# One load of a DMA-bound GroupNorm moved to the GpSimd queue, over fifteen DMA engines instead of sixteen

## The chip, the cores and the metric

The kernel runs on one core of one Trainium2 chip. The metric is the device time of one execution in microseconds (us). The page counts sixteen DMA engines on the core, and in the traces a large transfer posts sixteen landings whichever queue issues it (SyncE's stores below; GpSimd's load in the changed kernel, from 287.9 to 300.8 us).

## The reference

```python
# x: (128, 1024, 32, 16) bf16, G = 32 groups of 32 channels; g, b: (1024,)
xr = x.reshape(B, G, C // G, H, W)
mu = xr.mean(axis=(2, 3, 4), keepdims=True)
var = ((xr - mu) ** 2).mean(axis=(2, 3, 4), keepdims=True)
xn = (xr - mu) / jnp.sqrt(var + 1e-5)
return xn.reshape(B, C, H, W) * g[None, :, None, None] + b[None, :, None, None]
```

It reads 134 MB and writes 134 MB, and it computes little. Moving those bytes is the whole problem.

## The kernel before

The tensor is cut into 32 tiles of 128 rows (4 images times 32 groups). A row is 16,384 bf16 values, 32 KB in one piece. Six tile buffers rotate: five or six loads are in flight ahead of the computing, and a store releases a buffer for a load six tiles later. All large transfers go out on the SyncE queue.

```python
XBUFS = 6
UPFRONT = 6
AHEAD = 5
...
def L(i):                                   # load of tile i
    xt = xpool.tile([P, F], BF16, name="xt")
    parts = NQ if i == 0 or i >= NT - 1 else 1
    w = F // parts
    for c in range(parts):
        chain("sp", nc.sync.dma_start(out=xt[:, c*w:(c+1)*w], in_=x_v[i][:, c*w:(c+1)*w]))
    state[i] = {"xt": xt}
...
for i in range(NT):
    Q(i)                                    # ScalarE: sums of squares
    if i + 1 < NT:
        M(i + 1); R0(i + 1)                 # TensorE and VectorE: sums
    V(i)
    for c in range(NQ):
        A(i, c)                             # VectorE: 8 tensor_scalar of 128x512, in place
        ...
    if not in_parts:
        S(i, 0, NQ)                         # store of tile i, SyncE queue
    j = i + AHEAD
    if UPFRONT <= j < NT:
        L(j)
```

## Time and profile before

| | before |
|---|---|
| time, median of its first 3 runs | 638.12 us |
| DMA engines busy | 9 tenths or more in 39 of 40 slices |
| ScalarE, VectorE, TensorE busy | 79%, 65%, 45% |
| one row of 32 KB on one DMA engine | 1.213 us |

These lines are from the page of the kernel before: the span, the DMA busy row and the GB/s row (one entry for each fortieth of the span), the DMA queues, and the chain of work that ended last.

```profile
span 636.1 us, 3995 instructions
...
DMA  9999999999999999999999999999999999999993
GB/s 373 443 430 398 429 434 432 441 429 431 431 428 433 433 437 427 434 429 429 433 431 436 433 433 431 431 430 435 433 433 435 430 431 429 437 418 439 428 422 151
...
q1 hardware_dynamic: 10944, 268.44, 98.3%
q8 instruction: 8, 0.13, 0.1%
q14 instruction: 15, 0.12, 0.0%
...
DMA 80%; ACT 11%; issue 2%; DVE 2%; PE 1%; SPq 1%; DVEq 0%; ACTq 0%
```

The engines never rest and move about 430 GB/s in the middle of the run; q1 is the SyncE queue. q8 and q14 carry instructions, not data: 23 packets, a quarter of a megabyte.

An average over sixteen engines hides the one that is late. Every large transfer posts sixteen increments to its semaphore, and the trace has their times. They are read here as one from each engine: two loads in a row landed 9.7 us apart in all sixteen (22.4 to 22.8, then 32.1 to 32.5 us), which is eight rows of 1.213 us. In the fence below, the sixteen landing times in us, sorted, of three transfers of the kernel before (taken from the trace's landings, not a view of the page):

```
load landing first at  22.4:  22.4  22.4  22.4  22.4 ...  22.6  22.6  22.8
load landing first at 284.5: 284.5 284.6 284.6 284.8 ... 287.0 288.3 289.2 290.2
last store:                  623.7 623.8 624.0 624.2 624.3 625.3 625.6 625.6
                             625.7 625.8 625.9 626.5 628.1 628.8 628.8 635.1
```

The spread grows from 0.5 to 11.4 us. At the end one engine is alone, 6.3 us behind the next. The kernel ends when that one does.

### The profile page before, as it was taken

Reading aid. Unit: us, or ns where it says so; the run is one execution under the profiler, and the core shown is the slowest. Engines: PE = TensorE matmul, PEld = TensorE weight load, DVE = VectorE, ACT = ScalarE, POOL = GpSimd, SP = SyncE. Lnnn points to the kernel's source line nnn. Section 1 sums busy time; section 2 is a strip of 40 time slices with the busy share of each in tenths; the row PEclk is TensorE's granted clock in tenths of the full one; section 3 lists DMA queues with packets and bytes.
Section 4 is the critical chain, followed back from the end, with each engine's and each line's share of the span. In section 5 each row is a group of like instructions: output and inputs, shape, how many; then the busy total and the mean of one; then the engine's idle time right before and its main releaser. Section 6 shows DMA issues by size and latency. Waiting matters only on the chain.

```text
span 636.1 us, 3995 instructions
## 1 busy us (share of the span) xinstructions
PE 288.7 (45%) x1025; PEld 113.2 (18%) x1025; DVE 412.6 (65%) x1371; ACT 499.8 (79%) x298; POOL 0.8 (0%) x6
## 2 busy tenths in 40 slices
PE   5567604563335642356433555425553445546000
PEld 2223201221112210122111222112221112212000
DVE  1388888886686665875567756677555785668740
ACT  4899999997886777977679767797767986779920
POOL 0000000000000000000000000000000000000000
PEclk9789758766788666887567875678765787668655
DMA  9999999999999999999999999999999999999993
GB/s 373 443 430 398 429 434 432 441 429 431 431 428 433 433 437 427 434 429 429 433 431 436 433 433 431 431 430 435 433 433 435 430 431 429 437 418 439 428 422 151
DMA packets 11063, 268.70 MB, mean 422 GB/s; under 512 B 1312, under 2 KB 1312, under 8 KB 1312
## 3 DMA queue, kind: packets, MB, share of 16 engines
q1 hardware_dynamic: 10944, 268.44, 98.3%
q8 instruction: 8, 0.13, 0.1%
q14 instruction: 15, 0.12, 0.0%
q10 hardware_dynamic: 96, 0.00, 0.0%
HBM read 134.22 MB, written 134.22 MB: 422 GB/s over the span
## 4 chain that ended last, share of the span: by engine, by line
DMA 80%; ACT 11%; issue 2%; DVE 2%; PE 1%; SPq 1%; DVEq 0%; ACTq 0%
DMA out_dram<-xt 72%; ACT ja L228 11%; DMA xt<-in_x_dram 8%; DVE xt L305 1%; PE pa L162 1%; SPq L98 1%; DVE jv L245 0%; ACT rstd L258 0%; DVE rstd L266 0%; DVEq L372 0%; DVE bia L277 0%; DVE scl L271 0%; DVE jd L177 0%; ACTq L228 0%; SPq L318 0%
## 5 line engine op out<-in xcount | busy, mean ns | idle before, releaser
L228 ACT ACTIVATE ja<-xt,q 128x4096 bf16<-128x4096 bf16 x128 | 474.2, 3704 | 9.9 <-DVE jd L177 6.8
L305 DVE TENSOR_SCALAR xt<-xt,scl,bia 128x512 bf16<-128x512 bf16 x1016 | 333.5, 405 | 1.2
L162 PE MATMUL pa<-xt,eye 128*128 128x512 bf16 x256 | 109.8, 607 | 298.8 <-DMA xt<-in_x_dram 298.8
L162 PEld LDWEIGHTS <-eye 128*128 128x128 bf16 x1024 | 113.1, 113 | 474.4 <-DMA xt<-in_x_dram 300.2
L162 PE MATMUL pb<-xt,eye 128*128 128x512 bf16 x768 | 184.9, 400 | 1.0 <-DMA xt<-in_x_dram 1.0
L177 DVE TENSOR_SCALAR_CACHE_REDUCE jd<-pa 128x512 bf16<-128x512 f32 x32 | 22.1, 689 | 155.8 <-PE pa L162 155.8
L258 ACT ACTIVATE rstd<-var,eps_t 128x1 f32<-128x1 f32 x32 | 9.4, 294 | 96.4 <-DVE jv L245 96.4
L228 ACT ACTIVATION_READ_ACCUMULATOR ja<-xt,q 128x1 f32 x128 | 23.9, 186 | 0.0
L177 DVE TENSOR_SCALAR_CACHE_REDUCE jd<-pb,q 128x512 bf16<-128x512 f32 x32 | 23.7, 741 | 0.0
L245 DVE TENSOR_SCALAR_CACHE_REDUCE jv<-sq,seed 128x4 f32<-128x4 f32 x32 | 6.8, 214 | 18.9 <-ACT ja L228 18.9
L266 DVE RECIPROCAL rstd<-rstd 128x1 f32<-128x1 f32 x32 | 5.2, 164 | 11.6 <-ACT rstd L258 11.6
L277 DVE SCALAR_TENSOR_TENSOR bia<-scl,negmean,gb 128x32 f32<-128x32 f32 x32 | 8.0, 251 | 1.1
L271 DVE TENSOR_SCALAR scl<-gb,rstd 128x32 f32<-128x32 f32 x32 | 7.7, 242 | 1.1
L198 DVE TENSOR_SCALAR off<-negmean,q 128x1 f32<-128x1 f32 x32 | 6.8, 214 | 1.1
L298 ACT ACTIVATE xt<-xt,bia,scl 128x512 bf16<-128x512 bf16 x8 | 5.8, 800 | 0.8 <-DVE bia L277 0.8
L210 DVE SCALAR_TENSOR_TENSOR seed<-off 128x1 f32<-128x1 f32 x32 | 5.1, 159 | 1.1
L153 DVE COPY gb<-gb_p 128x64 f32<-128x64 f32 x1 | 0.2, 225 | 5.3 <-PE gb_p L145 5.3
L245 DVE DVE_READ_ACCUMULATOR jv<-sq,seed 128x1 f32 x32 | 2.6, 83 | 0.0
L177 DVE DVE_READ_ACCUMULATOR jd<-pa 128x1 f32 x32 | 2.6, 82 | 0.0
L113 ACT ACT_TABLE_LOAD x1 | 1.3, 1283 | 1.7 <-PEq L361 1.7
L177 DVE DVE_READ_ACCUMULATOR jd<-pb,q 128x1 f32 x32 | 2.5, 80 | 0.0
L111 DVE MEMSET eps_t<- 128x1 f32 x1 | 0.1, 59 | 0.9 <-PEq L361 0.9
(10 smaller groups left out, 1.7 us busy)
## 6 DMA issues: line engine op xcount, KB each, us to landing
xt<-in_x_dram SPq DMA_DIRECT2D x30, 4096.0 KB, 29.7
out_dram<-xt SPq DMA_DIRECT2D x30, 4096.0 KB, 39.1
xt<-in_x_dram SPq DMA_DIRECT2D x8, 1024.0 KB, 16.8
out_dram<-xt SPq DMA_DIRECT2D x8, 1024.0 KB, 25.3
gb_b<-in_g_dram ACTq DMA_DIRECT2D x1, 2.0 KB, 3.3
gb_b<-in_b_dram ACTq DMA_DIRECT2D x1, 2.0 KB, 5.3
```

The costliest lines, as they stand in the source:

```text
L98: nc.sync.dma_start(out=xt[:, c * w : (c + 1) * w], in_=x_v[i][:, c * w : (c + 1) * w]),
L162: nc.tensor.matmul(out=ps[:], lhsT=eye[:], rhs=st["xt"][:, k * MMN : (k + 1) * MMN], start=(k == lo), stop=(k == hi - 1),),
L177: nc.vector.tensor_scalar(out=jd[:], in0=ps[:], scalar1=-inv_n, scalar2=seed, op0=ALU.mult, op1=ALU.add, accum_out=total[:],),
L198: nc.vector.tensor_scalar(out=off[:], in0=st["negmean"][:], scalar1=1.0 / NQ, scalar2=st["q"][:], op0=ALU.mult, op1=ALU.subtract,),
L228: nc.scalar.activation(out=ja[:], in_=st["xt"][:, k * QF : (k + 1) * QF], func=ACT.Square, bias=st["q"][:], scale=1.0 / NQ, accum_out=sq[: ...
L245: nc.vector.tensor_scalar(out=jv[:], in0=st["sq"][:], scalar1=inv_n, scalar2=st["seed"][:], op0=ALU.mult, op1=ALU.add, accum_out=var[:],),
L258: nc.scalar.activation(out=rstd[:], in_=var[:], func=ACT.Sqrt, bias=eps_t[:], scale=float(NQ * NQ),),
L266: chain("dve", nc.vector.reciprocal(out=rstd[:], in_=rstd[:]))
L271: nc.vector.tensor_scalar(out=scl[:], in0=gam, scalar1=rstd[:], scalar2=None, op0=ALU.mult),
L277: nc.vector.scalar_tensor_tensor(out=bia[:], in0=scl[:], scalar=st["negmean"][:], in1=bet, op0=ALU.mult, op1=ALU.add,),
L298: nc.scalar.activation(out=span, in_=span, func=ACT.Identity, bias=bia, scale=scl),
L305: nc.vector.tensor_scalar(out=span, in0=span, scalar1=scl, scalar2=bia, op0=ALU.mult, op1=ALU.add,),
```

## The change

The intent is to give the late engine less to do. Each engine normally carries eight of a tile's 128 rows (the 9.7 us above). For tile 16, rows 0 to 119 are issued from GpSimd, meant for fifteen engines with eight rows each, so that one takes none; rows 120 to 127 go out from SyncE. Two tiny loads of the weights `g`, whose data nobody reads, are there to set which engine GpSimd's load leaves out.

```diff
+SPLIT_TILE = 16
+WIDE = 120
+SPARED = 4
...
+    def turn(n):
+        t = consts.tile([n, 4, 4], BF16, name=f"turn{n}")
+        chain("pool", nc.gpsimd.dma_start(
+            out=t[:, :, 0:2],
+            in_=g[0 : n * 8].rearrange("(p a c) -> p a c", a=4, c=2)))
+
     def L(i):
         xt = xpool.tile([P, F], BF16, name="xt")
+        if i == SPLIT_TILE:
+            chain("pool", nc.gpsimd.dma_start(
+                out=xt[0:WIDE, :], in_=x_v[i][0:WIDE, :], max_dma_last_dim=F))
+            chain("sp", nc.sync.dma_start(out=xt[WIDE:P, :], in_=x_v[i][WIDE:P, :]))
+            turn(16 - SPARED)
+            state[i] = {"xt": xt}
+            return
...
     for i in range(min(UPFRONT, NT)):
         L(i)
+
+    turn(SPARED + 1)
```

More of the change, by code (lines that the diff above doesn't have):

```diff
@@ L89 @@
     state = {}
+    def turn(n):
+        t = consts.tile([n, 4, 4], BF16, name=f"turn{n}")
+        chain(
+            "pool",
+            nc.gpsimd.dma_start(
+                out=t[:, :, 0:2],
+                in_=g[0 : n * 8].rearrange("(p a c) -> p a c", a=4, c=2),
+            ),
+        )
     def L(i):
         xt = xpool.tile([P, F], BF16, name="xt")
+        if i == SPLIT_TILE:
+            chain(
+                "pool",
+                nc.gpsimd.dma_start(
+                    out=xt[0:WIDE, :], in_=x_v[i][0:WIDE, :], max_dma_last_dim=F
+                ),
+            )
+            chain("sp", nc.sync.dma_start(out=xt[WIDE:P, :], in_=x_v[i][WIDE:P, :]))
+            turn(16 - SPARED)
+            state[i] = {"xt": xt}
+            return
         parts = NQ if i == 0 or i >= NT - 1 else 1
```

## The prediction

The places marked as cut, here and in the expectations below, held statements that no trace or run of this case shows: how queues choose their engines, what in the hardware makes rows slow each other, and what a load from GpSimd might cost.

> **What bounds the kernel now.** The DMA engines. On the page, the busy row is 9 in 39 of 40 slices, q1 fills 98.3% of 16 engines' span at a mean 422 GB/s, and the chain of work that ended last is 80% DMA, 11% ACT. ACT (79%) and DVE (65%) have slack.
>
> The sixteen engines are not alike. Every large transfer posts sixteen landings in the trace. They spread over 0.5 us at the first tiles, 5.7 us by 290 us, and 11.4 us at the last store: first 623.7, then 628.1, 628.8, 628.8, and one alone at 635.1. So one engine is 6.3 us behind the next two, and the program waits for it. Its lag grows in steps of about 1 us (at 251, 310, 360, 418, 468, 527, 576 us); the 8 KB instruction packets of q14 start just before (242, 301, 358, 416, 459, 517, 574 us). I read it as the engine that fetches one compute engine's instructions. Packets carry no engine number; followed end to start, the late engine was the fifth to start, which fits engine 4 but proves nothing.
>
> **What the change does.** Each engine moves 8 rows of 32 KB per tile, 1.213 us a row. For tile 16, 120 rows go from GpSimd over fifteen engines, 8 each; the last 8 rows from SyncE. [...] So engine 4 carries 1 row instead of 8: 7 x 1.213 = 8.5 us less[...]. No run here shows this placement yet[...].
>
> **Critical path.** All of the late engine's excess is on it. After, the late engine ends at 635.1 - 8.5 = 626.6; the next, 628.8 (630.0 with an extra row), becomes last. Gain at most 5.1 to 6.3 us.
>
> Costs: [...] A late start of this load hurts little: its tile's store is issued about 49 us after it lands (290 to 339 us), while computing takes about 29. The engines then hold at least 8 us of queued work, so none should starve.
>
> **Prediction.** 633.8 us (-0.7%); 80% range 631.2 to 639.5. Faster by over 2%: 1%; within 2%: 98%; slower by over 2%: 1%.
>
> **What would show it.** Right: after the load of tile 16 the gap between last and second-last landing (1.7 us at 310) vanishes; the last store's gap falls from 6.3 to under 1.5 us; the first landings move under 2 us. The GpSimd load lands within 35 us of issue.
>
> **What would make it wrong.** Engine 4 is not the late one[...]: the gap stays about 6 us and the time is 638 to 640. Or GpSimd's load is slow[...]: all sixteen landings shift by several microseconds and the gain is eaten.

In numbers, the forecast's sum was 638.1 us, less the gain of 5.1 to 6.3 us, plus a cost of 1 to 2 us on every engine: 632.8 to 635.0, put at 633.8. The cost term came from no run. The extra row of 1.213 us, for the eight engines that take the last eight rows, is in the 630.0. That engine 4 takes one row was an assumption too; the traces showed later that the eight-row load posts its landings at 279.2, 284.7 to 286.3 (six of them) and 295.3 us, the engine that runs ahead and the late one among them. As for the 8 us of queued work, the trace of before has 13.6 us for the earliest engine at 280.6 us, when the load of the next tile was issued: it ended its part of the last transfer queued by then at 294.2.

## The result, and the profile after

The changed kernel took 642.83 us (median of 4 runs, 641.93 to 643.41), against 638.11 us before (4 runs): a ratio of 1.0072, 95% interval 1.0054 to 1.0089. Ratios here are the mean time of one kernel's fast runs over that of the other's fast runs of the same rounds, so they are not quite the ratio of the medians. The outcome is within 2%, but on the wrong side, and outside the predicted range.

The same lines of the page of the changed kernel:

```profile
span 641.7 us, 4006 instructions
...
DMA  9999999999999999999999999999999999999992
GB/s 382 433 424 406 437 426 428 434 439 427 427 433 437 429 431 434 421 358 411 436 429 428 438 433 429 431 436 431 429 436 435 432 429 431 435 418 440 424 426 106
...
q1 hardware_dynamic: 10816, 264.51, 96.3%
q0 software_dynamic: 336, 3.93, 1.7%
q8 instruction: 8, 0.13, 0.1%
q14 instruction: 15, 0.12, 0.0%
...
DMA 79%; ACT 11%; issue 2%; PE 2%; DVE 2%; SPq 1%; DVEq 0%; ACTq 0%
```

The busy row is as full as before, and the chain by engines reads the same to a per cent. (By lines it doesn't: it now runs through tile 16's load, and the loads' share of it is 14% instead of 8%.) The GB/s row shows a dent in slices 17 to 19 (421, 358, 411), where tile 16 is loaded; q0 is GpSimd's queue. The view of busy time by stretches says where in the dent. Its columns are the stretch, its length, then TensorE, weight load, VectorE, ScalarE and GpSimd busy, the granted clock, the DMA busy share and GB/s; here before:

```profile
262.00:278.00 16.00, 7.11 (x24) 2.84 (x25) 9.46 (x33) 11.93 (x8) 0.00 (x0) 0.68 1.00 430
278.00:288.00 10.00, 2.08 (x10) 0.76 (x8) 9.93 (x32) 9.90 (x7) 0.00 (x0) 0.87 1.00 429
288.00:300.00 12.00, 9.75 (x32) 3.72 (x32) 5.67 (x21) 8.09 (x6) 0.00 (x0) 0.68 1.01 434
```

and after:

```profile
262.00:278.00 16.00, 3.00 (x9) 1.04 (x8) 7.43 (x24) 10.29 (x6) 1.33 (x2) 0.59 1.00 417
278.00:288.00 10.00, 5.92 (x26) 2.40 (x24) 8.68 (x30) 8.28 (x6) 0.00 (x0) 0.97 1.02 324
288.00:300.00 12.00, 0.00 (x0) 0.00 (x0) 4.29 (x14) 7.11 (x4) 0.00 (x0) 0.53 0.96 397
```

From 278 to 288 us the engines are 100% busy and move 324 GB/s instead of 429. Busy is not moving: the engines count as busy and move a quarter less. What slows them is tested below.

The landings of the changed kernel, from its trace (us; the store of tile 12 was issued at 262.5, just before GpSimd's load):

```
store of tile 12: 289.1 297.6 297.7 298.2 ... 301.0 301.4 305.6
last store:       627.7 628.4 628.5 628.7 628.7 628.9 629.3 629.6
                  629.7 630.0 630.1 630.3 630.3 630.8 631.1 640.7
```

Two things can be read here. First, one engine is 8.5 us ahead of the next (289.1 to 297.6): an engine has been spared. That the lead equals what was meant (7 rows of 1.213 us) is partly chance: the same store landed from 294.2 to 299.9 us before, so the others had lost some 3 us by now, and the probes below show that the spared engine used to be about 2 us behind the first. Secondly, it was the wrong one: the late engine is still there, and its gap to the next has grown to 9.6 us (640.7 to 631.1). And the others are later too: the middle of the sixteen last landings (mean of the eighth and ninth) moved from 625.65 to 629.65, by 4.0 us, and the late engine by 5.6 us.

So there are two questions. Which engine is late, and which was spared? And what costs the others 4 us?

### The profile page after: what moved, and what is told of

Read it like the earlier page. It is cut to its first block, busy times and chain, and to the rows that moved or that the text cites. A ratio compares the mean times of both kernels' runs of the same rounds, so it can differ in the third digit from the quotient of the medians.

```text
span 641.7 us, 4006 instructions
## 1 busy us (share of the span) xinstructions
PE 290.0 (45%) x1025; PEld 113.3 (18%) x1025; DVE 412.9 (64%) x1371; ACT 499.9 (78%) x298; POOL 2.8 (0%) x9
## 4 chain that ended last, share of the span: by engine, by line
DMA 79%; ACT 11%; issue 2%; PE 2%; DVE 2%; SPq 1%; DVEq 0%; ACTq 0%
DMA out_dram<-xt 65%; DMA xt<-in_x_dram 14%; ACT ja L255 11%; PE pa L189 2%; DVE xt L332 1%; SPq L123 1%; DVE jv L272 0%; ACT rstd L285 0%; DVE scl L298 0%; DVE jd L204 0%; DVE rstd L293 0%; DVEq L399 0%; DVE bia L304 0%; SPq L345 0%; SPq L114 0%
## 5 line engine op out<-in xcount | busy, mean ns | idle before, releaser
L189 PE MATMUL pb<-xt,eye 128*128 128x512 bf16 x768 | 186.8, 403 | 1.0 <-DMA xt<-in_x_dram 1.0
## 6 DMA issues: line engine op xcount, KB each, us to landing
xt<-in_x_dram POOLq DMA_DIRECT2D x1, 3840.0 KB, 38.2
```

What stands on the lines that cost most here:

```text
L189: nc.tensor.matmul(out=ps[:], lhsT=eye[:], rhs=st["xt"][:, k * MMN : (k + 1) * MMN], start=(k == lo), stop=(k == hi - 1),),
```

## The experiments

Theories on the first question: (A) engine 4 was spared as meant and the late one is another; (B) engine 4 is the late one and GpSimd's choice stood elsewhere. On the second: (C) GpSimd's queue itself; (D) the new row layout: engines that write certain rows of a tile at the same time slow each other.

### Which engine is which: tiny loads as probes

A SyncE load of n rows of 4 bytes posts n landings (three for n = 3 in the fence below, five for n = 5). Queued behind a big load, it tells when each of its n engines got there. The probes rest on the assumption that each load takes the engines of the one before and one more; an engine whose lag (or lead) first appears at n is then called number n - 1, counted from 0. All numbers of engines below are meant so.

```diff
+        pn = i - PROBE_FROM        # 7 in probe_before, 16 in probe_after
+        if 1 <= pn <= PROBES:
+            pt_ = consts.tile([pn, 2], BF16, name=f"probe{pn}")
+            chain("sp", nc.sync.dma_start(
+                out=pt_[:], in_=g[0 : 2 * pn].rearrange("(p c) -> p c", c=2)))
```

> The kernel before, plus one tiny load (n rows of 4 bytes, n = 1 to 16) on the SyncE queue right behind the load of tile n+7; each posts n landings[...]. Theory A (the change spared the engine it meant to, but engine 4 is not the late one): the late engine's landing time, several us behind the rest, first appears at some n other than 5, and since the late engine showed up among the eight landings of the 8-row load in the changed kernel, at an n of 8 or less. Theory B (engine 4 is the late one[...]): it first appears at n = 5. If the late landing appears at every n or in no order, rows are not placed by number and neither can be told. Time within 1 us of before.

> The changed kernel, plus the same tiny loads (n = 1 to 12) behind the loads of tiles 17 to 28. Theory A: the engine that runs about 2 us ahead of all others after tile 16 first appears at n = 5, the late one at the n that the other probe finds. Theory B: the early one first appears elsewhere, the late one at n = 5. Time within 1 us of the changed kernel, 642 to 644 us.

The probe on the kernel before took 638.34 us (one run), the probe on the changed one 641.87 us, just below the 642 expected. Their landings (us; "load" is the last part of the load right ahead of the probe):

```
kernel before:  load ... 169.82 171.29 172.24 172.32   n=3: 168.60 168.71 169.44
                load ... 189.73 190.76 191.72 192.68   n=4: 187.97 188.08 188.82 192.86
                load ... 209.35 210.49 211.32 212.05   n=5: 207.35 207.45 208.25 209.23 212.24
changed kernel: load 362.45 364.17 ... 369.27 373.64   n=4: 366.69 366.96 368.80 373.84
                load 381.89 383.56 ... 388.58 392.98   n=5: 382.08 386.04 386.32 388.12 393.16
```

The late engine appears first at n = 4, 4.0 us behind the next, and is there again at n = 5: it is number 3. The engine that runs ahead in the changed kernel, by 4.0 us, appears first at n = 5: number 4 was spared. The assumption agrees with the loads shown. Theory A holds. The eight-row load then made matters worse for engine 3: its landing is among the eight of that load (295.3 us, 9.0 us behind the next), so it got a ninth row.

### GpSimd's queue by itself

```diff
         if i == SPLIT_TILE:
-            (120 rows from GpSimd, 8 rows from SyncE, both turns)
+            chain("pool", nc.gpsimd.dma_start(out=xt[:], in_=x_v[i], max_dma_last_dim=F))
```

> Tile 16 loaded whole by GpSimd: 128 rows over sixteen engines[...], no 8-row load on SyncE. If the cost of some 4 to 5 us on every engine comes from GpSimd's queue itself ([...]smaller 16 KB pieces, two queues taking turns), it stays: 641 to 643 us. If it comes from the 8-row load on the SyncE queue, whose rows 120 to 127 lie close together, or from the fifteen-engine layout, it goes: 638 to 639 us, and no load packet of 32 KB takes over 2.3 us.

It took 638.94 us (ratio 1.0004, interval 0.9988 to 1.0021). Theory C falls: GpSimd's queue costs nothing measurable. Of its 256 pieces of 16 KB, 254 took under 0.7 us (median 0.611). The stretch that was slow after is at full speed:

```profile
278.00:288.00 10.00, 6.01 (x24) 2.36 (x22) 9.46 (x33) 9.20 (x6) 0.00 (x0) 0.84 1.01 433
```

### The eight rows on SyncE

In the changed kernel, six of the SyncE queue's packets of 32 KB that began between 279.7 and 281.1 us took 2.27 to 3.21 us instead of 1.21. They fit the eight-row load, six of whose landings came from 284.7 to 286.3 us: eight engines write eight neighbouring rows there at the same time. In pairs8 the same rows go out two at a time, four apart.

```diff
-            chain("sp", nc.sync.dma_start(out=xt[WIDE:P, :], in_=x_v[i][WIDE:P, :]))
+            for r in range(4):      # rows 120 and 124, 121 and 125, ...
+                chain("sp", nc.sync.dma_start(
+                    out=xt[WIDE + r : P : 4, :], in_=x_v[i][WIDE + r : P : 4, :]))
```

> The changed kernel, with the last eight rows in four loads of two rows, four apart (120 and 124, 121 and 125, ...), so that two engines carry four rows each instead of eight engines one row each. If the eight rows jam[...] (in the changed kernel six such packets took 2.3 to 3.2 us instead of 1.2), the stretch from 278 to 288 us keeps its speed, all landings move 2 to 3 us earlier and the time is 637.5 to 640 us unless the late engine is one of the two. If the cost is GpSimd's queue or the fifteen-engine layout, it stays at 641 to 644 us.

It took 640.74 us (ratio 1.0040, interval 1.0025 to 1.0055), at the edge above what D expected (637.5 to 640) and just below the 641 of its rival. The slow stretch recovers most of its speed:

```profile
278.00:288.00 10.00, 6.11 (x27) 2.49 (x25) 8.49 (x30) 8.09 (x6) 0.00 (x0) 0.96 0.99 390
```

390 GB/s, after 324 in the changed kernel; one packet near there is still over 2.3 us, at 2.38. The late engine's last landing came at 637.6 us, 3.1 us before the changed kernel's. It should have no ninth row here (SyncE's loads are of two rows now, and the probe with n = 3 has no late landing yet), which is worth 1.2 us; the remaining 1.9 us is the jam's share. That is by one profiled run of each kernel; by the medians (642.83 and 640.74) they differ by 2.1 us, which leaves 0.9 for the jam. Some 2.5 us over the 635.1 of before are left, with the fifteen-engine layout the remaining suspect. Its mark is in the trace: 52 of GpSimd's 240 pieces took over 0.7 us here, against 2 of 256 in gp128.

### The split without GpSimd

```diff
-            chain("pool", nc.gpsimd.dma_start(
-                out=xt[0:WIDE, :], in_=x_v[i][0:WIDE, :], max_dma_last_dim=F))
+            chain("sp", nc.sync.dma_start(out=xt[0:WIDE, :], in_=x_v[i][0:WIDE, :]))
             chain("sp", nc.sync.dma_start(out=xt[WIDE:P, :], in_=x_v[i][WIDE:P, :]))
-            turn(16 - SPARED)
...
-    turn(SPARED + 1)
```

> The same split of tile 16 (120 rows and 8 rows) all from the SyncE queue, no GpSimd load[...]. If the cost comes from the split[...] and not from GpSimd: 641 to 644 us, as the changed kernel, with the last landing 4 us or more later than before. If two queues taking turns on one engine are needed for the cost: 638 to 640 us.

It took 649.34 us (ratio 1.0172, interval 1.0147 to 1.0197): slower than expected under either theory. The split alone, without GpSimd, costs 11 us. The page's DMA rows and two stretches:

```profile
DMA  9999999999999999999999999999999999999993
GB/s 388 424 419 418 428 433 435 426 436 430 428 440 426 432 437 423 436 262 357 422 442 429 424 442 430 422 440 430 430 437 430 433 428 432 436 419 437 422 420 147
...
278.00:288.00 10.00, 1.71 (x8) 0.59 (x6) 9.93 (x32) 9.90 (x7) 0.00 (x0) 0.81 1.02 249
288.00:300.00 12.00, 0.00 (x0) 0.00 (x0) 0.06 (x1) 2.92 (x2) 0.00 (x0) 0.50 0.94 270
```

Of the SyncE queue's 32 KB packets that began from 262 to 300 us, 83 took over 2.3 us, and 62 of these between 2.3 and 2.6: twice 1.213. So many rows of the split load took twice as long; what in the hardware does it isn't shown by any run. In the changed kernel the same split cost far less. There GpSimd's pieces took turns with rows of a store, which read SBUF and do not write it, so only about half of the engines were writing at a time (GpSimd's pieces were under way on 6.2 of sixteen, on average, from 270 to 288 us). That is an explanation that fits the two traces; no run isolates the taking of turns.

### The layout alone: 64 rows against 32

```diff
+        if i == SPLIT_TILE:        # in the kernel before
+            for lo, hi in ((32, 96), (0, 32), (96, 128)):
+                chain("sp", nc.sync.dma_start(out=xt[lo:hi, :], in_=x_v[i][lo:hi, :]))
+            state[i] = {"xt": xt}
+            return
```

The first outcome named is that of theory D.

> The kernel before, with tile 16 loaded from SyncE in three pieces in a row: rows 32 to 95, then 0 to 31, then 96 to 127; no GpSimd, nobody spared. If the slow rows come from two engines[...], the 64-row piece[...] runs at about 1.21 us a row and the two 32-row pieces[...] at about 2.43 us: some 64 packets near 2.4 us, every engine about 4.9 us later, time 642 to 644 us. If any load that is not 128 rows is slow, all 128 packets take about 2.4 us and the time is 647 to 649 us. If neither, 638 to 639 us.

It took 644.44 us (ratio 1.0091, interval 1.0076 to 1.0106), just above the 642 to 644 expected. By the first landing of each transfer, the store ahead ended at 275.0 us, the 64-row piece at 279.7 (four rows in 4.7 us: full speed), the first 32-row piece at 286.1 (two rows in 6.4 us) and the second at 291.2 (two rows in 5.1 us). 59 packets took over 2.3 us, against 64 expected; the four rows that took 4.7 us together cannot be among them. So it isn't that any load of fewer than 128 rows is slow: the same queue, in a row, is at full speed with rows 32 to 95 in one piece and at less than half of it with 32 rows in one. Theory D holds, in that the rows that go out together set the speed; what in the hardware slows them isn't shown. The slow rows took 2.3 to 3.7 us, some more than the double of 1.21; why is open. The dent in the stretch view:

```profile
278.00:288.00 10.00, 1.93 (x9) 0.69 (x7) 9.93 (x32) 9.90 (x7) 0.00 (x0) 0.85 1.08 223
```

### Why engine 3 is late

```diff
+    pad = consts.tile([P, 1], F32, name="pad")
     def A(i, c):
+        for _ in range(PAD // NQ):      # PAD = 16
+            chain("dve", nc.vector.memset(pad[:], 0.0))
```

> The kernel before with 16 tiny memsets of one element more per tile on VectorE: 512 instructions[...], some 30 us of VectorE time where it idles over 200 us. If the late engine is late because it fetches VectorE's instructions (8 KB a time, about 1 us each): about four more q14 packets of 8 KB, gap between last and second-last landing near 10 us instead of 6.3, time 641 to 643 us. If its lag has another cause: 638 to 639 us.

It took 641.15 us (ratio 1.0045, interval 1.0030 to 1.0059). The q14 line of its page, 15 packets before:

```profile
q14 instruction: 19, 0.16, 0.1%
```

Its last landings were 628.4, 629.4 and 638.6 us, the first still 623.7: the other engines are where they were, the late one is 3.5 us later and its gap has grown from 6.3 to 9.2 us, for four more packets of 8 KB (32 KB, or 64 bytes for each of the 512 instructions). The late engine is late because it also fetches VectorE's instructions, at nearly 1 us a packet, of which the packet itself is 0.31 us; the rest is a slower row behind it (1.86 us instead of 1.21 for the rows begun at 241.9, 301.0 and 358.8 us in the kernel before).

### Sparing engine 3

```diff
-SPARED = 4
+SPARED = 3
```

> The changed kernel with SPARED = 3 instead of 4, nothing else. The tiny loads showed the late engine at n = 4, that is number 3 counted from 0, and the spared one at n = 5, number 4. Theory A (off by one, with a cost of some 4 us on all other engines): engine 3 lands about 8.5 us earlier than in the changed kernel and is no longer last; engine 4, now with nine rows, becomes last or near it. Last landing 633 to 636 us instead of 640.7, gap between last and second-last under 2.5 us instead of 9.5, time 635.5 to 639 us. If the late engine is not a fixed engine but moves with the program, the gap stays over 6 us and the time 641 to 644.

It took 638.31 us (ratio 1.0000, interval 0.9983 to 1.0017): in the range expected, 4.5 us less than the changed kernel by the medians, and no better than before. The last gap was expected under 2.5 us and is not. The gap of the last engine after tile 16 is 0.3 us at 310.9 and 0.2 us at 340.1. It opens again to 4.2 us by the end (634.8 to 630.6), in good part by a steady 0.2 us a store from about 360 us on. No other run shows such a creep, and which engine it is and why isn't known.

### Engine 3 spared, and the eight rows in pairs from GpSimd

```diff
 (SPARED = 3; turn() counts its tiles for unique names)
-            chain("sp", nc.sync.dma_start(out=xt[WIDE:P, :], in_=x_v[i][WIDE:P, :]))
-            turn(16 - SPARED)
+            for r in range(4):
+                turn(12 if r == 0 else 14)
+                chain("pool", nc.gpsimd.dma_start(
+                    out=xt[WIDE + r : P : 4, :], in_=x_v[i][WIDE + r : P : 4, :],
+                    max_dma_last_dim=F))
```

> SPARED = 3, and the last eight rows no longer as one load from SyncE but as four loads of two rows from GpSimd[...]. If the eight-row jam and the wrong engine are the two faults: no load packet of 32 KB over 2.3 us near 280 us, last landing 630 to 632.5 us, time 632.5 to 635.5 us, faster than before by 0.4 to 0.9%. If the cost sits elsewhere (fifteen-engine layout alone): 636 to 639 us.

It took 637.03 us (ratio 0.9972, interval 0.9950 to 0.9993), in the range of the rival and short of the 632.5 to 635.5 hoped for. The last store landed between 626.8 and 634.1, with a last gap of 1.4 us: the late engine is gone as such, but the middle is at 629.1, 3.5 us later than before. The cost of the layout was still paid: 50 of the 256 pieces took over 0.7 us, against 2 in gp128, where the same queue has the 128-row layout. A second fault came with the pairs: GpSimd waited 31.0 us for an earlier load's semaphore before it issued the last pair at 298.4 us, so tile 16 landed at 325.7 us instead of 290.2 and the compute engines stood idle from 300 to 324 us. The DMA engines stayed busy meanwhile (429 GB/s from 312 to 324 us); whether this wait cost time as well was not separated from the layout.

### Rows chosen so as not to jam

```diff
 (SPARED = 3)
+            rows("pool", nc.gpsimd, slice(32, 92))          # meant: fifteen engines, 4 rows each
+            for r in range(4):
+                rows("sp", nc.sync, slice(r, 32, 4))
+            for r in range(2):
+                rows("sp", nc.sync, slice(92 + r, 96, 2))
+            for r in range(4):
+                turn(5 if r == 0 else 8)
+                rows("pool", nc.gpsimd, slice(96 + r, P, 4))
```

GpSimd's 60 rows are to be four to an engine, as in the 64-row piece; the rest goes out every fourth or second row. The first outcome named is for the case that the layout is what was left of the cost.

> SPARED = 3 again,[...] rows 32 to 91 from GpSimd over fifteen engines (four rows each), rows 0 to 31 in four SyncE loads of every fourth row[...], rows 96 to 127 likewise from GpSimd[...], rows 92 to 95 in two SyncE pairs[...]. Engine 3 moves four rows less, 4.85 us. [...] all packets near 0.61 and 1.21 us, the first landing of the last store back within 1.5 us of before's 623.7, the last at 630 to 632, time 633 to 635.5 us. If the many small loads cost as much themselves: 636 to 639 us.

It took 636.50 us (ratio 0.9968, interval 0.9952 to 0.9985), again short of what was hoped (633 to 635.5). The part about the layout came true: no 32 KB packet of the SyncE queue near there took over 1.8 us, 12 of 184 GpSimd pieces took over 0.7 us, and the middle of the last landings is 626.95, only 1.3 us later than before; the first is at 624.8, within the 1.5 us allowed. What was wrong is the last one, 634.0 instead of 630 to 632: engine 3 was to be given back only four rows, the two engines of the pairs from rows 92 to 95 got two more each, and which of them it is was not probed. Tile 16 also landed late, at 309.6 instead of 290.2 us, since GpSimd waited 15.2 us for an earlier load before it issued the last of its small ones; the chain of waits of this run goes through it.

Both of the last two kernels beat the kernel before by about 0.3%, and by their medians the changed kernel by about 1%. Against the 6.3 us between the late engine and the next that is little.

| kernel | time, us (median) | middle of last landings | last landing |
|---|---|---|---|
| before (profiled run) | 638.1 | 625.65 | 635.1 |
| changed | 642.83 | 629.65 | 640.7 |
| gp128 | 638.94 | 626.0 | 636.7 |
| pairs8 | 640.74 | 627.2 | 637.6 |
| sync120 | 649.34 | 635.0 | 645.4 |
| sync64_32 | 644.44 | 632.95 | 642.4 |
| dve_pad | 641.15 | 625.55 | 638.6 |
| spare3 | 638.31 | 628.3 | 634.8 |
| spare3_pairs | 637.03 | 629.1 | 634.1 |
| ports_apart | 636.50 | 626.95 | 634.0 |

The second and third columns are from the one profiled run of each, so differences of about 1 us in them can be chance: gp128, as fast as before, has a last landing 1.6 us later, and its profiled run was its slowest of four. Medians of before lay between 638.11 and 638.52 us.

The slow packets account for the shift of the middle. Add up what the packets begun from 262 to 315 us took beyond 1.213 us (32 KB, SyncE) and beyond 0.611 us (16 KB, GpSimd), and divide by sixteen engines: 3.7 us in the changed kernel, 1.9 in pairs8, 0.6 in gp128, 9.4 in sync120 and 7.2 in sync64_32. The middles moved by 4.0, 1.5, 0.3, 9.3 and 7.3 us. (It fits less well in spare3_pairs, 2.3 against 3.5, and ports_apart, 0.7 against 1.3, the two runs with many small loads.) Of the 59 us in the changed kernel 31 lie in GpSimd's pieces, which have 0.3 us in gp128.

## Why the prediction was wrong

- "Engine 4 is the late one". This step failed. The prediction took it from the order in which packets began, called it no proof, and still built its main figure on it. The probes showed number 3. The fifth engine to start is not engine 4; the prediction treated an order in time as a number. An unspared late engine was in its list of what would make it wrong, priced at 638 to 640 us, without the ninth row that this engine then got.
- The 1 to 2 us on every engine for the other costs. This term was mis-sized: the middle moved by 4.0 us and the late engine by 5.6. It was a guess about GpSimd's load and the layout of its 120 rows. It did not see that the last eight rows, counted as 1.2 us on each of eight engines, would slow each other (2.27 to 3.21 us for six of the packets). The jam was worth 1 to 2 us on the late engine (pairs8, less the ninth row), and the layout of the 120 rows about 2 us (1.9 us by the slow packets of pairs8, 2.5 by its last landing).
- The two failures were priced one at a time. The ninth row (1.2 us), the jam and the layout together make 4 to 5 us, against 4.7 us between the medians and 5.6 us between the last landings of the two profiled runs. The top of the range, 639.5, left room for one of the two failures.
- The bound was read correctly: the program ends with its latest DMA engine, and that engine is late for its instruction fetches (dve_pad: +3.5 us for four packets, the others unmoved).
- The placement was right: engine 4 was spared (probe_after) and ran 8.5 us ahead of the next (289.1 to 297.6 us).
- "A late start of this load hurts little" was right: tile 16 landed 10.6 us later than before (300.8 for 290.2; 38.2 us after its issue, not within the 35 predicted), and the engines that mattered had work. "None should starve" was wrong for one: engine 4, the spared one, had ended its part of the store of tile 12 at 289.1 us, and SyncE issued the next load at 293.1, when the late engine had at last freed a buffer.
- The gain expected if the right engine were spared, 5.1 to 6.3 us less 1 to 2, did not come either: spare3 gained nothing over before. There the middle is 2.65 us later, which its slow packets explain (2.7 us by the same sum), and one engine that nobody identified ends 4.2 us behind the next; why the second happened isn't known.

## What to carry to other kernels

In a kernel that keeps all DMA engines busy, look at the sixteen landings of single transfers and not at the mean busy share: the latest engine sets the end, and a full busy row can hide rows that take twice as long (sync120 from 278 to 288 us: DMA share 1.02, 249 GB/s for the 429 of before). Before an engine is spared by number, find its number with a load of n rows, for n from 1 up. When a transfer is cut differently from 128 rows, look at what one row takes in the trace: 1.21 us here in loads of 128 rows and in the 64-row piece, 2.3 us and more for many rows of the loads of 120, 32 and 8; eight rows in the wrong place cost more here than the whole queue change.
